# A fused attention and two-MLP kernel: the second MLP by seven block products in place of eight

## The chip, the cores and the metric

One NeuronCore of a Trainium2 chip runs the whole program. The metric is the device time of one execution in microseconds; the kernel before takes 1175.07 us (median of 3 runs, 1174.54 to 1177.42).

## What is computed

Four batches of eight heads of attention (576 positions, head size 64, scores masked to those within `tau` of the row's maximum), then two MLPs in float32 over 2304 tokens of width 512:

```python
x = attention(q, k, v, tau)                  # 2304 x 512
h = x @ w_in;  y = (h * sigmoid(h)) @ w_out  # 512 -> 2048 -> 512
out = ((y @ w_a) * (y @ w_b)) @ w_out2       # 512 -> 1536 -> 512
```

The MLP weights reach the kernel as 64-bit words (float64). They are turned on chip into a pair of float32r matrices, a high part and a low part, and each product is made of three matmuls: low weight by high activation, high by high, high weight by low activation.

## The kernel before

**Order of the work.** The body does not issue instructions directly. It records tasks in a planner (`Plan.add`) with an engine, a cost, a rank, what they wait for and which buffer ring they take, and `Plan.run` plays them through and so fixes the order in which each engine's instructions stand. On the chip every engine then takes its own list strictly in that order, and waits at an instruction until its inputs are there. Tasks of the second MLP's weights have the rank 1e6, so the plan puts them where an engine has nothing else.

**First MLP.** Tokens go in five blocks of 256 and two of 512 (`BLOCKS`), each in 16 steps of 128 hidden columns. `mlp1_up` does 12 matmuls into one PSUM bank (`hb` or `hc`), ACT takes tanh, DVE the gate `th` (L743), ACT the high part `gh`, DVE the low part `gl` (L749), and `mlp1_down` does 12 matmuls of the step before into the banks `yc` to `yf` or `sb`. At a block's end the result is halved, stored to DRAM as `yT_d` (L816) and read back by `load_y` of the second MLP. Blocks 0 to 3 run amid the attention; `closed` marks its end. Block 4 and the two big blocks come after it: the late part.

**Second MLP's weights.** `split_weight` makes one 128x512 piece at a time, 36 in all, from `closed` on: load, two ACT passes (low word L330, high part L354), DVE scale, sign and join (L337, L341, L346), an integer add of two words on POOL (L350) and the low part on POOL or DVE (L358). The pieces stay in SBUF, in the 32 tiles `w` that the first MLP's weights leave one by one, and in 4 more.

**Second MLP.** Tokens go in four blocks of 512 and one of 256. For each of 12 slices of 128 hidden columns `mlp2_up` does 24 matmuls of the block's width (L876, banks `ps_a` and `ps_b`); ACT copies a, DVE multiplies by b (L886), ACT and DVE split the product (L889, L892); `mlp2_down` does 3 matmuls of 512 columns for each 128 tokens (L920) into `op`. In all 1152 matmuls of 512 columns and 288 of 256 in the up part, 648 of 512 in the down part.

Of the kernel before, what the change touches and what calls it, by code (L numbers as in the profile page):

```python
# [21 lines left out]
P = 128  # L22
# [12 lines left out]
T2 = 512  # L35

# [178 lines left out]
def fused_kernel(ctx: ExitStack, tc: tile.TileContext, qk, qk2, v, tau, w_in, w_out, w_a, w_b, w_o2, out):  # L215
# [14 lines left out]
    yT_d = dram.tile([NC, P, NT], F32, name="yT_d")  # L230

# [3 lines left out]
    def pool(stack, name, bufs, side="left", **kw):  # L235
# [18 lines left out]
    xb_p = pool(p1, "xb", RINGS["xb"])  # L254
    g_p = pool(p1, "g", 2)
    yo_p = pool(p1, "yo", RINGS["yo"])
# [121 lines left out]

    def w1_chunk(i, rank):
        j, i = divmod(i, 8)  # L380
        engines = dict(scale_engine=SCALE_ON[i % len(SCALE_ON)], lo_engine=LO_ON[i % len(LO_ON)], most=PIECE)
        if i < 4:
            return split_weight(("in", i, j), w_in[i * P:(i + 1) * P, j * 512:(j + 1) * 512], rank, "w", **engines)
        f = 4 * j + i - 4
        return split_weight(("out", f), w_out[f * P:(f + 1) * P, :], rank, "w", **engines)
# [446 lines left out]
    y2, y2_ready, zs, z_ready, o_ps = {}, {}, {}, {}, {}  # L832

    def load_y(t0):
        tn = min(T2, NT - t0)
        need = [t for a, m, t in y_dma if a < t0 + tn and a + m > t0]
        ab = "ab"[t0 // T2 % 2]

        def split(c):
            s = {}  # L840

            def load():
                s["r"] = pools["ya"].tile([P, T2], F32, name="yr", bufs=RINGS["yr"])
                nc.sync.dma_start(out=s["r"][:, :tn], in_=yT_d[c, :, t0:t0 + tn])

            def hi():
                s["h"] = pools["y" + ab].tile([P, T2], F32R, name="yh" + ab)
                s["l"] = pools["y" + ab].tile([P, T2], F32R, name="yl" + ab)
                y2[t0, c] = (s["h"], s["l"])
                nc.scalar.copy(out=s["h"][:, :tn], in_=s["r"][:, :tn])  # L850

            def lo():
                nc.vector.tensor_sub(out=s["l"][:, :tn], in0=s["r"][:, :tn], in1=s["h"][:, :tn].bitcast(F32))

            ld = dma(-1, P * 4 * tn, load, after=[*need, closed], take=["yr"])
            h = pl.add("ACT", act_ns(tn), R_AUX, hi, [ld], ["y2" + ab], behind=[closed1] if ab == "b" else [])
            l = pl.add("DVE", dve_ns(tn), R_AUX, lo, [h])
            pl.free("yr", l)
            y2_ready[t0, c] = (h, l)

        for c in range(NC):
            split(c)

    def mlp2_up(n, t0, f):
        tn = min(T2, NT - t0)
        s = zs[t0, f] = {}

        def up(nm, c):
            def fn():
                if c == 0:  # L870
                    s[nm] = pools["ab", n % 2].tile([P, T2], F32, name=f"ps_{nm}")
                w = wt[nm, c, f // 4]
                o = (f % 4) * P
                yh, yl = y2[t0, c]
                for k, (a, yy) in enumerate(((1, yh), (0, yh), (0, yl))):
                    nc.tensor.matmul(s[nm][:, :tn], lhsT=w[:, a, o:o + P], rhs=yy[:, :tn],  # L876
                                     start=(c == 0 and k == 0), stop=(c == NC - 1 and k == 2))
            return fn
# [9 lines left out]
        def hi():  # L888
            nc.scalar.copy(out=s["zh"][:, :tn], in_=s["z"][:, :tn])  # L889
# [166 lines left out]
```

## Time and profile before

| what | value |
|---|---|
| median of 3 runs | 1175.07 us |
| span of the profiled execution | 1173.2 us |
| PE busy | 1142.9 us, 97% |
| DVE busy | 621.7 us, 53% |
| ACT busy | 531.1 us, 45% |
| POOL busy | 271.4 us, 23% |
| DMA traffic | 90.05 MB, mean 77 GB/s |

The profiled execution is given by its span, from its first to its last instruction; the run times are taken by another clock around the whole execution and lie 1.9 us above it at the median. A busy share is an average over stages: attention until about 497 us, the late part of the first MLP until about 725 us, the second MLP to the end. A matmul's record runs on after the next has started, so the pace of matmuls is read from their starts, not from their durations.

### The profile page before, as it was taken

To read this page: it belongs to the slowest core of one execution; us is meant where nothing else is said; L and a number is where in the kernel's file an instruction comes from. 1 tells how busy PE (TensorE), PEld (TensorE's weight loads), DVE (VectorE), ACT (ScalarE), POOL (GpSimd) and SP (SyncE) were. 2 spreads that over 40 slices of the span, in tenths; PEclk is the share of its full clock that TensorE was granted. 3 is DMA by queue.
4 is the path that set the end of the run, shared out by engine and by line. 5 is a ranking of instruction groups with operands and counts; after the bars stand their busy time and mean duration, and the time that the engine had idled before them with its cause. 6 is when DMAs were issued, how large, how long until landed. Compare 5 with 4: busy or idle time off the path is not lost.

```text
span 1173.2 us, 18253 instructions
## 1 busy us (share of the span) xinstructions
PE 1142.9 (97%) x6917; PEld 957.8 (82%) x6917; DVE 621.7 (53%) x1416; ACT 531.1 (45%) x999; POOL 271.4 (23%) x440
## 2 busy tenths in 40 slices
PE   8789989999999999999999999999999999999998
PEld 6456757988999989899888888888888888888897
DVE  8988887877777777463223678673211311211121
ACT  7877786666766766442223445442211211211121
POOL 2444444333322422140001344451000000000000
PEclk9999999999999999999999999999999999999999
DMA  6654543322322221150001235440100200000000
GB/s 199 199 163 138 163 155 109 113 88 79 107 73 84 82 95 35 36 190 18 1 1 45 88 111 167 140 138 13 63 1 1 68 0 1 23 28 1 1 36 18
DMA packets 41095, 90.05 MB, mean 77 GB/s; under 512 B 4256, under 2 KB 18224, under 8 KB 41008
## 3 DMA queue, kind: packets, MB, share of 16 engines
q1 hardware_dynamic: 40864, 88.89, 23.7%
q8 instruction: 54, 0.88, 0.3%
q14 instruction: 33, 0.27, 0.1%
q10 hardware_dynamic: 144, 0.00, 0.0%
HBM read 74.65 MB, written 14.23 MB: 76 GB/s over the span
## 4 chain that ended last, share of the span: by engine, by line
PE 60%; DMA 2%; DVE 1%; ACT 1%; issue 0%; POOL 0%; SPq 0%; ACTq 0%; POOLq 0%
PE ps_a L876 13%; PE op L920 13%; PE ps_b L876 13%; PE hb L730 5%; PE hc L730 4%; PE sb L790 3%; PE yc L790 2%; PE yd L790 1%; PE ye L790 1%; PE yf L790 1%; DMA wraw<-w_a 1%; PE av L605 1%; PE tp L560 1%; PE sa L495 1%; DMA wraw<-w_b 1%
## 5 line engine op out<-in xcount | busy, mean ns | idle before, releaser
L886 DVE TENSOR_TENSOR z<-ps_b,z 128x512 f32<-128x512 f32 (+1 forms) x60 | 38.2, 637 | 227.9 <-PE ps_b L876 227.8
L730 PE MATMUL hb<-xh,w 128*128 128x256 f32 (+1 forms) x704 | 155.2, 310 | 1.5 <-DVE th L743 1.0
L350 POOL TENSOR_TENSOR wt<-wc,wt 128x128 uint32<-128x128 uint32 (+1 forms) x164 | 111.2, 702 | 140.2 <-DVE wc L346 98.7
L920 PE MATMUL op<-w,zh 128*128 128x512 f32 x432 | 133.9, 391 | 0.0
L511 DVE TENSOR_SCALAR_CACHE_REDUCE t<-sa,nscale 128x576 f32<-128x576 f32 x128 | 103.7, 810 | 50.6 <-PE sa L495 45.6
L528 DVE SCALAR_TENSOR_TENSOR e<-t,thr,e 128x576 f32<-128x576 f32 x128 | 111.5, 871 | 26.4 <-ACT e L525 24.8
L730 PEld LDWEIGHTS hb<-xh,w 128*128 128x128 f32 x704 | 113.0, 190 | 10.9 <-issue 2.3
L560 PE MATMUL tp<-ident,e 128*128 128x128 f32 x706 | 106.2, 278 | 12.9 <-DVE e L528 8.3
L560 PEld LDWEIGHTS tp<-ident,e 128*128 128x128 f32 x706 | 78.7, 140 | 37.2 <-issue 14.7
L525 ACT ACTIVATE e<-t,min 128x576 f32<-128x576 f32 x128 | 99.9, 781 | 19.2 <-DVE t L511 18.5
L883 ACT COPY z<-ps_a 128x512 f32<-128x512 f32 (+1 forms) x60 | 32.6, 543 | 165.0 <-PE ps_a L876 165.0
L730 PE MATMUL hb<-xl,w 128*128 128x256 f32 (+1 forms) x352 | 106.5, 303 | 0.7 <-POOL xl L702 0.7
L790 PE MATMUL sb<-gh,w 128*128 128x256 f32 (+1 forms) x576 | 97.6, 300 | 0.0
L920 PEld LDWEIGHTS op<-w,zh 128*128 128x128 f32 x432 | 80.3, 188 | 16.4
L889 ACT CAST zh<-z 128x512 fp32r<-128x512 f32 (+1 forms) x60 | 34.7, 578 | 127.5 <-DVE z L886 127.5
L790 PEld LDWEIGHTS sb<-gh,w 128*128 128x128 f32 x576 | 80.0, 190 | 5.9 <-issue 3.3
L920 PE MATMUL op<-w,zl 128*128 128x512 f32 x216 | 84.6, 392 | 0.0
L749 DVE TENSOR_TENSOR gl<-th,gh 128x256 fp32r<-128x256 f32 (+1 forms) x112 | 63.9, 571 | 28.3 <-ACT gh L746 28.1
L876 PE MATMUL ps_a<-yha,w 128*128 128x512 f32 (+1 forms) x288 | 77.4, 355 | 0.0
L876 PE MATMUL ps_b<-yha,w 128*128 128x512 f32 (+1 forms) x288 | 77.0, 354 | 0.0
L640 POOL TENSOR_TENSOR x<-x,xi 128x128 f32<-128x128 f32 (+2 forms) x80 | 40.9, 535 | 147.1 <-issue 49.9
L702 POOL TENSOR_TENSOR xl<-xr,xh 128x128 fp32r<-128x128 f32 x72 | 37.0, 542 | 161.0 <-ACT xh L699 156.4
(123 smaller groups left out, 2342.8 us busy)
## 6 DMA issues: line engine op xcount, KB each, us to landing
qk<-qk SPq DMA_DIRECT2D x20, 576.0 KB
wraw<-w_in SPq DMA_DIRECT2D x16, 512.0 KB
wraw<-w_out SPq DMA_DIRECT2D x16, 512.0 KB
v<-v SPq DMA_DIRECT2D x20, 320.0 KB
wraw<-w_a SPq DMA_DIRECT2D x12, 512.0 KB
wraw<-w_b SPq DMA_DIRECT2D x12, 512.0 KB
wraw<-w_o SPq DMA_DIRECT2D x12, 512.0 KB
out<-ob SPq DMA_DIRECT2D x18, 256.0 KB
```

Of the source, the lines that this page charges most:

```text
L350: nc.gpsimd.tensor_tensor(out=s["t"][:, o], in0=s["c"][:, o].bitcast(U32), in1=s["t"][:, o], op=ALU.add)
L511: nc.vector.tensor_scalar(out=s["t"], in0=s["s"][:, :, :NH], scalar1=nscale, scalar2=None, op0=ALU.mult, op1=ALU.min, accum_out=s["min"])
L525: nc.scalar.activation(out=s["e"], in_=s["t"], func=AF.Exp, scale=-1.0, bias=s["min"])
L528: nc.vector.scalar_tensor_tensor(out=s["e"], in0=s["s"][:, :, :NH] if early else s["t"], scalar=s["thr"], in1=s["e"], op0=ALU.is_ge if ear ...
L560: nc.tensor.transpose(t["tp"][:, j * P:(j + 1) * P], e["e"][:, o:o + P], ident)
L640: nc.gpsimd.tensor_tensor(out=s["x"][:, o], in0=s["x"][:, o], in1=s["i"][:, o], op=ALU.mult)
L730: nc.tensor.matmul(s["h"], lhsT=w[:, a, o:o + P], rhs=xx, start=(c == 0 and k == 0), stop=(c == NC - 1 and k == 2))
L749: nc.vector.tensor_sub(out=s["gl"], in0=s["t"], in1=s["gh"].bitcast(F32))
L790: nc.tensor.matmul(ys[j][e // per][:, e % per * tn:(e % per + 1) * tn], lhsT=w[:, a, e * P:(e + 1) * P], rhs=gs[j, f][g], start=(f == 0 an ...
L876: nc.tensor.matmul(s[nm][:, :tn], lhsT=w[:, a, o:o + P], rhs=yy[:, :tn], start=(c == 0 and k == 0), stop=(c == NC - 1 and k == 2))
L886: nc.vector.tensor_mul(out=s["z"][:, :tn], in0=s["b"][:, :tn], in1=s["z"][:, :tn])
L920: nc.tensor.matmul(o_ps[t0, i], lhsT=s[z][:, i * P:(i + 1) * P], rhs=wt["o2", f][:, a, :], start=(f == 0 and k == 0), stop=(f == NF2 - 1 a ...
```

## The change

The second MLP is done with Strassen's scheme in Winograd's form. Both matrices of each product are cut in 2 x 2 blocks; seven products of block sums replace eight of blocks. A unit is 768 tokens, and its two halves are the even and the odd tokens, 384 each (`TN`).

- **Weights.** In place of 36 pieces there are 36 units of four blocks (`split_unit`): 24 for `w_a` and `w_b`, 12 for `w_out2`. ACT does three passes (L870, L873, L898), DVE everything else: sign, join, the integer add (`total`), three small sums (`combine`, `both`), and the low part of seven blocks (`lo`, 896 columns). POOL does none of it. The seven blocks, high and low, are stored to DRAM (`wab_d`, `wo_d`) by one DMA of 917,504 bytes that is cut in pieces of 512 bytes; the load is two DMAs in pieces of 1 KB. Units go through buffers `u` (two deep) and, in the big blocks, also `v`.
- **Stream.** For every product (up) or third of a product (down) 512 KB of weights, 4 KB a partition, are read back from DRAM into one of 12 tiles `ws`: 63 loads per unit of tokens, 189 in all.
- **Products.** `products` runs them in the order 1, 6, 5, 7, 2, 4, 3 over three pairs of PSUM banks and keeps partial sums in the banks. After 1 ACT copies a pair out; after 6, 7, 5, 4 and 3 DVE adds (`u2`, `v`, `c22`, `c21`, `c12`, 768 columns each). Product 7 waits for `u2`, 4 for `v`, 3 for `c22`. Each up product is 12 matmuls of 384 columns, each down product three times 12.
- **Token sums.** `load_y` reads 768 tokens at once and DVE makes four block sums; the seven operands are split by ACT and DVE (`halves`). In the down part each third of a product needs one such split, through rings `zh` and `zl` of two tiles.
- **Start.** `closed1`, which opens the second MLP's tiles, stands behind all 36 stores.
- **Output.** `out` is written transposed, and the host puts it in order.

```diff
+UNIT = 768
+TN = UNIT // 2
+NG = NF2 // 2
+ORDER = (1, 6, 5, 7, 2, 4, 3)
+CHAIN = {1: 0, 2: 0, 6: 1, 7: 1, 4: 1, 5: 2, 3: 2}
+PART = {1: 0, 4: 1, 2: 2, 5: 3, 6: 4, 7: 5, 3: 6}
+N_YW, N_SW, N_TW = 14, 12, 6
+SPARE = range(6, 30)
+LO2_ON = ("DVE",)
+TOTAL_ON = ("DVE",)
...
+    wab_d = dram.tile([NG, 7, P, 2, 4, P], F32, name="wab_d")
+    wo_d = dram.tile([7, NG // 2, P, 2, 2, 2, P], F32, name="wo_d")
...
+    def split_unit(key, src, dst, rank, lane, behind, lo_engine, total_engine):
...
+        def low():
+            s["a"] = new("s", [P, 8, P], F32)
+            nc.scalar.activation(out=s["a"][:, 4:].bitcast(U32), in_=s["raw"][:, :, :, 0], func=AF.Copy, scale=2.0**-29)
+
+        def scale():
+            nc.scalar.activation(out=s["a"][:, :4], in_=s["raw"][:, :, :, 1].bitcast(F32), func=AF.Copy, scale=2.0**-112)
+
+        def sign():
+            nc.vector.tensor_scalar(out=s["raw"][:, :, :, 1], in0=s["raw"][:, :, :, 1], scalar1=0x80000000, scalar2=None,
+                                    op0=ALU.bitwise_and)
+
+        def join():
+            c = s["a"][:, :4].bitcast(U32)
+            nc.vector.scalar_tensor_tensor(out=c, in0=c, scalar=3, in1=s["raw"][:, :, :, 1],
+                                           op0=ALU.logical_shift_left, op1=ALU.bitwise_or)
+
+        def total(o):
+            a = s["a"].rearrange("p a n -> p (a n)").bitcast(U32)
+            eng = nc.gpsimd if total_engine == "Pool" else nc.vector
+            eng.tensor_tensor(out=a[:, o], in0=a[:, o], in1=a[:, 512 + o.start:512 + o.stop], op=ALU.add)
+
+        def combine(o, x, y, op):
+            return lambda: nc.vector.tensor_tensor(out=s["a"][:, o], in0=s["a"][:, x], in1=s["a"][:, y], op=op)
+
+        def both():
+            a = s["a"]
+            nc.vector.tensor_tensor(out=a[:, 4:6], in0=a[:, 0:7:6], in1=a[:, 2:3].broadcast_to((P, 2, P)), op=ALU.add)
+
+        def hi():
+            s["w"] = new("w", [P, 2, 7, P], F32R)
+            nc.scalar.copy(out=s["w"][:, 0], in_=s["a"][:, 1:])
+
+        def lo():
+            eng = nc.gpsimd if lo_engine == "Pool" else nc.vector
+            eng.tensor_tensor(out=s["w"][:, 1], in0=s["a"][:, 1:], in1=s["w"][:, 0].bitcast(F32), op=ALU.subtract)
+
+        def store():
+            nc.sync.dma_start(out=dst.rearrange("i p l n -> p l i n"), in_=s["w"].bitcast(F32))
...
+        a = dma(rank, P * 4096, load, n=2, take=[lane + "r"], behind=behind)
+        l = pl.add("ACT", ac(512), rank, low, [a], take=[lane + "s"])
+        c = pl.add("ACT", ac(512), rank, scale, [a], behind=[l])
+        h = pl.add("DVE", 600, rank, sign, [a, c], port=True)
+        j = pl.add("DVE", dv(512), rank, join, [h, c], port=True)
+        pl.free(lane + "r", j, l)
+        if total_engine == "Pool":
+            t = on_pool(512, rank, total, [j, l], PIECE)[-1]
+        else:
+            t = pl.add("DVE", dv(512), rank, lambda: total(slice(0, 512)), [j, l], port=True)
+        t = pl.add("DVE", dv(P), rank, combine(6, 0, 1, ALU.subtract), [t], port=True)
+        t = pl.add("DVE", dv(2 * P), rank, both, [t], port=True)
+        t = pl.add("DVE", dv(P), rank, combine(7, 3, 5, ALU.subtract), [t], port=True)
+        i = pl.add("ACT", ac(7 * P), rank, hi, [t], [lane + "w"])
+        o = pl.add(lo_engine, pool_ns(7 * P) if lo_engine == "Pool" else dv(7 * P), rank, lo, [i], port=True)
+        pl.free(lane + "s", o)
+        st = dma(rank, P * 7168, store, after=[o], slack=SLACK)
+        pl.free(lane + "w", st)
+        stored[key] = st
+        return st
...
+            lane, behind = ("v", [closed_x]) if n % 3 == 2 and n in SPARE else ("u", [closed])
...
+    def stream(src, after):
+        s = {}
+
+        def load():
+            s["w"] = pools["ws"].tile([P, 2, 512], F32R, name="w")
+            nc.sync.dma_start(out=s["w"].bitcast(F32), in_=src)
+
+        s["ready"] = dma(1e4 + pe_at[0], P * 4096, load, after=after, take=["ws"])
+        return s
...
+    def products(s, do, after):
+
+        p, cost = {}, 12 * pe_ns(TN)
+        p1, u2, v, c22, c21, c12 = chain(s)
+        add = lambda fn, deps, take=(): pl.add("DVE", dv(UNIT), -3, fn, deps, take)
+        wait = {}
+        for i in ORDER:
+            take, behind, alloc = [], [], None
+            if i in (1, 6, 5):
+                alloc, behind = take_pair(s, CHAIN[i])
+                take = ["pr"]
+            for k, (fn, deps, done) in enumerate(do(i)):
+                def run(fn=fn, alloc=alloc if k == 0 else None):
+                    if alloc:
+                        alloc()
+                    fn()
+                p[i] = pe_task(cost, run, [*deps, *wait.get(i, ())], take if k == 0 else [], behind if k == 0 else [])
+                done(p[i])
+            if i == 1:
+                wait_p1 = pl.add("ACT", ac(UNIT), -3, p1, [p[1]], ["tm"], behind=[closed1])
+                wait[2] = [wait_p1]
+            elif i == 6:
+                s["u2"] = add(u2, [p[6], wait_p1], ["tm"])
+                wait[7] = [s["u2"]]
+            elif i == 7:
+                s["v"] = add(v, [p[7]], ["tm"])
+                s["c22"] = add(c22, [s["v"], p[5]])
+                wait[4], wait[3] = [s["v"]], [s["c22"]]
+            elif i == 2:
+                after(p[2])
+            elif i == 4:
+                s["c21"] = add(c21, [p[4], s["v"]])
+            elif i == 3:
+                s["c12"] = add(c12, [p[3]])
+        return p
...
+    def mlp2_up(u, g, y):
...
+                bank = s["b", CHAIN[i]]
+                for m in range(2):
+                    for k in range(2):
+                        for q, (a, x) in enumerate(((1, "h"), (0, "h"), (0, "l"))):
+                            nc.tensor.matmul(bank[:, m, :TN], lhsT=w["w"][:, a, (2 * m + k) * P:(2 * m + k + 1) * P],
+                                             rhs=y[i][x][:, k, :TN], start=(i in (1, 6, 5) and k == 0 and q == 0),
+                                             stop=(k == 1 and q == 2), skip_group_check=True)
+            yield fn, [w["ready"], *y[i]["ready"]], lambda p: pl.free("ws", p)
...
+    def mlp2_down(u):
...
+                z = halves(lambda k=k, sl=sl: zs[u, sl, k][:, :, :TN], TN,
+                           lambda: pools["zc"].tile([P, 2, TN], F32R, name="zh", bufs=RINGS["zh"]), "zh",
+                           lambda: pools["zc"].tile([P, 2, TN], F32R, name="zl", bufs=RINGS["zl"]), "zl",
+                           [zs[u, sl, "ready"][i]], 1e4 + pe_at[0] + sl)
...
+    closed_x = pl.add("none", 1, 0, close_small, behind=[small_done, closed])
...
+    closed_y = pl.add("none", 1, 0, close_spare, behind=prepare_weights())
+    closed1 = pl.add("none", 1, 0, close_mlp1,
+                     behind=[up_last[0], down_last[0], closed_x, closed_b, *stored.values(), *(t for *_, t in y_dma)])
+    for u in range(NT // UNIT):
+        y = load_y(u, pe_at[0])
+        for g in range(NG):
+            p = mlp2_up(u, g, y)
+        for i in ORDER:
+            pl.free("wy", p[i])
+            pl.free("wy", p[i])
+        mlp2_down(u)
```

How the engines' lists move, at three places. DVE, a step and a half of the first MLP's last block, in the kernel before (`th` is the gate, `gl` the low part; `wraw`, `wc`, `w` are a weight piece):

```order
L743 SCALAR_TENSOR_TENSOR th_8765<-th_8765,hc 128x512
L341 TENSOR_SCALAR wraw<-wraw 128x512
L749 TENSOR_TENSOR gl_8767<-th_8765,gh_8766 128x512
L346 SCALAR_TENSOR_TENSOR wc<-wc,wraw 128x512
L337 TENSOR_SCALAR wc<-wraw 128x512
L341 TENSOR_SCALAR wraw<-wraw 128x512
L358 TENSOR_TENSOR w<-wt,w 128x512
L743 SCALAR_TENSOR_TENSOR th_8814<-th_8814,hb 128x512
```

DVE in the same block now, from one gate to the next (`us`, `ur`, `uw` are one unit's buffers; the integer add is the row `ISA`):

```order
L760 SCALAR_TENSOR_TENSOR th_8837<-th_8837,hb 128x512
L894 TENSOR_TENSOR us<-us 128x256
L881 SCALAR_TENSOR_TENSOR us<-us,ur 128x512
L766 TENSOR_TENSOR gl_8839<-th_8837,gh_8838 128x512
L890 TENSOR_TENSOR us<-us 128x128
L887 ISA us<-us 128x1024
L890 TENSOR_TENSOR us<-us 128x128
L902 TENSOR_TENSOR uw<-us,uw 128x896
L894 TENSOR_TENSOR us<-us 128x256
L760 SCALAR_TENSOR_TENSOR th_8890<-th_8890,hc 128x512
```

Between two gates stand seven instructions of weights where five stood. The first of them in DVE's list comes right behind block 3's last evacuation; the last comes just ahead of the last step's gate. In between stand 36 units of weights, 31 gates and low parts of 512 columns, 15 and 16 of 256, 3 evacuations, and 11 operations of 768 columns on the first unit of tokens. Ahead of that place the lists of all engines are the same as before.

PE in the second MLP, one group of 128 + 128 hidden columns (`pr` are pairs of banks):

```order
L1120 MATMUL pr_9566<-w 128x384 x12
L1120 MATMUL pr_9584<-w 128x384 x12
L1120 MATMUL pr_9605<-w 128x384 x12
L1120 MATMUL pr_9584<-w 128x384 x12
L1120 MATMUL pr_9566<-w 128x384 x12
L1120 MATMUL pr_9584<-w 128x384 x12
L1120 MATMUL pr_9605<-w 128x384 x12
L1120 MATMUL pr_9694<-w 128x384 x12
```

The seven products follow each other with nothing between, 1512 matmuls in all; the down part has 756. Before, an up step of 24 matmuls and a down step of 12 took turns.

DVE in the down part of the first unit of tokens (`zl` is the low part of a product's operand):

```order
L975 TENSOR_TENSOR zl<-z_9428,zh 128x768
L1056 TENSOR_TENSOR tm<-pr_10143,tm 128x768
L975 TENSOR_TENSOR zl<-z_9675,zh 128x768
L1059 TENSOR_TENSOR tm<-pr_10215,tm 128x768
L975 TENSOR_TENSOR zl<-z_9922,zh 128x768
L975 TENSOR_TENSOR zl<-w,zh 128x768 x3
```

A low part now stands ahead of every 12 matmuls, with at most one other operation between two of them.

## Rows read from the trace of the kernel before

**Rows 1.** The page: span, busy time by engine, granted TensorE clock in 40 slices.

```profile
span 1173.2 us, 18253 instructions
PE 1142.9 (97%) x6917; PEld 957.8 (82%) x6917; DVE 621.7 (53%) x1416; ACT 531.1 (45%) x999; POOL 271.4 (23%) x440
PEclk9999999999999999999999999999999999999999
```

**Rows 2.** The chain that ended last, share of the span by engine.

```profile
PE 60%; DMA 2%; DVE 1%; ACT 1%; issue 0%; POOL 0%; SPq 0%; ACTq 0%; POOLq 0%
```

**Rows 3.** Busy time by stretch: PE, PEld, DVE, ACT, POOL, clock, DMA share, GB/s.

```profile
540.00:726.00 186.00, 185.95 (x859) 155.30 (x858) 88.94 (x133) 67.25 (x114) 38.72 (x38) 1.00 0.18 56
726.00:1169.00 443.00, 443.00 (x2081) 370.26 (x2079) 129.57 (x206) 100.60 (x179) 36.47 (x27) 1.00 0.12 39
```

**Rows 4.** Timeline of PE: the second MLP's first, a late first-MLP, the last matmul.

```profile
723.17 0.63 PE L876 MATMUL ps_a<-yha,w 128*128 128x512 f32 x2
...
723.87 0.40 PE L790 MATMUL yc<-gl,w 128*128 128x512 f32 x1
...
1168.97 0.39 PE L920 MATMUL op<-w,zl 128*128 128x512 f32 x1
```

**Rows 5.** Timeline of PE, block 4: two rows that lie 24 matmuls apart.

```profile
520.80 0.64 PE L790 MATMUL yc<-gh,w 128*128 128x256 f32 x4
...
523.68 0.64 PE L790 MATMUL yc<-gh,w 128*128 128x256 f32 x4
```

**Rows 6.** Groups by line and shape, DVE and ACT, 820 to 1160 us.

```profile
L892 DVE TENSOR_TENSOR zl<-z,zh 128x512 fp32r<-128x512 f32 x37 | 25.6, 693 | 23.4 <-ACT zh L889 23.3
L892 DVE TENSOR_TENSOR zl<-z,zh 128x256 fp32r<-128x256 f32 x10 | 4.2, 424 | 4.2 <-ACT zh L889 4.2
L889 ACT CAST zh<-z 128x512 fp32r<-128x512 f32 x36 | 22.4, 621 | 99.4 <-DVE z L886 99.4
L889 ACT CAST zh<-z 128x256 fp32r<-128x256 f32 x10 | 4.1, 406 | 14.7 <-DVE z L886 14.7
```

**Rows 7.** Timeline of DVE and POOL, 721 to 726 us.

```profile
721.20 1.83 DVE L749 TENSOR_TENSOR gl<-th,gh 128x512 fp32r<-128x512 f32 x1
721.19 1.29 POOL L350 TENSOR_TENSOR wt<-wc,wt 128x512 uint32<-128x512 uint32 x1 [1.56 <-DVE wc L346]
723.89 0.41 DVE L341 TENSOR_SCALAR wraw<-wraw 128x512 uint32<-128x512 uint32 x1
724.34 0.69 DVE L346 SCALAR_TENSOR_TENSOR wc<-wc,wraw 128x512 uint32<-128x512 uint32 x1
724.95 0.68 DVE L812 TENSOR_SCALAR yo<-yd 128x512 f32<-128x512 f32 x1
```

**Rows 8.** Timelines of SP, DVE and PE: the ends of the late part's stretches.

```profile
497.90 0.43 SPq L326 DMA_DIRECT2D wraw<-w_a  x1
505.95 0.69 DVE L812 TENSOR_SCALAR yo<-sb 128x512 f32<-128x512 f32 x1 [0.18 <-ACT yo L810]
718.06 0.39 PE L730 MATMUL hc<-xl,w 128*128 128x512 f32 x1
```

**Rows 9.** DMA, 545 to 560 us: two stores in 1 KB pieces (packets, MB, share).

```profile
q1 hardware_dynamic: 544, 0.52, 10.3%
```

**Rows 10.** DMA, 638 to 646 us: four stores in 2 KB pieces.

```profile
q1 hardware_dynamic: 576, 1.05, 35.1%
```

**Rows 11.** DMA, 488.2 to 489.2 us: one store of five 512-byte pieces.

```profile
q1 hardware_dynamic: 10, 0.00, 1.1%
```

**Rows 12.** DMA, 497.4 to 500 us: loads of 4 KB pieces, nearly alone.

```profile
q1 hardware_dynamic: 384, 0.70, 92.1%
```

**Rows 13.** DMA, 729 to 732 us: loads of 4 KB and 2 KB pieces, nearly alone.

```profile
q1 hardware_dynamic: 542, 1.16, 104.9%
```

**Rows 14.** Timelines of ACT and SP: the last evacuation and the last stores' issue.

```profile
1169.40 0.58 ACT L927 COPY ob<-op 128x512 f32<-128x512 f32 x1 [1.83 <-PE op L920]
1169.43 0.91 SPq L931 DMA_DIRECT2D out<-ob  x2
```

More of the change, by code (lines that the diff above doesn't have):

```diff
@@ L377, in split_weight, with w_pool @@
         return [a, l, c, h, j, *ts, i, *os]
+    def w_pool(k):
+        return "wy" if k < N_YW else "ws" if k < N_YW + N_SW else "wz"
     def w1_chunk(i, rank):
+        dst = w_pool(i)
         j, i = divmod(i, 8)
@@ L829, in mlp1_down @@
                 b_done.extend(evs[2:])
[L832 to L862, printed above, removed]
@@ new lines, in prepare_weights @@
+    def prepare_weights():
+        units = []
+        for g in range(NG):
+            for m, w in enumerate((w_a, w_b)):
+                for k in range(2):
+                    r = w.rearrange("(h k p) (e f) two -> h k p e f two", h=2, k=2, e=2)
+                    units.append(((m, k, g), [r[h, k, :, :, g * P:(g + 1) * P] for h in range(2)], wab_d[g, :, :, :, 2 * m + k]))
+        for g in range(NG):
+            for c in range(2):
+                r = w_o2.rearrange("(h g p) (e f) two -> h g p e f two", h=2, g=NG, e=2)
+                units.append((("o", g, c), [r[h, g, :, :, c * P:(c + 1) * P] for h in range(2)], wo_d[:, g // 2, :, :, g % 2, c]))
+        done = []
+        for n, unit in enumerate(units):
+            lane, behind = ("v", [closed_x]) if n % 3 == 2 and n in SPARE else ("u", [closed])
+            st = split_unit(*unit, 1e6 + n, lane, behind, LO2_ON[n % len(LO2_ON)], TOTAL_ON[n % len(TOTAL_ON)])
+            if lane == "v":
+                done.append(st)
+        return done
@@ new lines, in fused_kernel, with pe_task, load @@
+    pe_at = [0]
+    pe_last = [None]
+    def pe_task(cost, fn, after, take=(), behind=()):
+        pe_at[0] += 1
+        pe_last[0] = pl.add("PE", cost, 1e5 + pe_at[0], fn, after, take, behind=[pe_last[0], *behind])
+        return pe_last[0]
+    def stream(src, after):
+        s = {}
+        def load():
+            s["w"] = pools["ws"].tile([P, 2, 512], F32R, name="w")
+            nc.sync.dma_start(out=s["w"].bitcast(F32), in_=src)
+        s["ready"] = dma(1e4 + pe_at[0], P * 4096, load, after=after, take=["ws"])
+        return s
@@ new lines, in halves, with hi, lo @@
+    def halves(v, n, hi_pool, hi_take, lo_pool, lo_take, after, rank, behind=()):
+        s = {}
+        def hi():
+            s["h"] = hi_pool()
+            nc.scalar.copy(out=s["h"][:, :, :n], in_=v())
+        def lo():
+            s["l"] = lo_pool()
+            nc.vector.tensor_sub(out=s["l"][:, :, :n], in0=v(), in1=s["h"][:, :, :n].bitcast(F32))
+        h = pl.add("ACT", ac(2 * n), rank, hi, after, [hi_take], behind=behind)
+        l = pl.add("DVE", dv(2 * n), rank, lo, [h], [lo_take])
+        s["ready"] = [h, l]
+        return s
@@ L979, in fused_kernel, with close_small @@
             mlp1_down(n - 1, *units[n - 1])
+        if n and units[n - 1] == (4, NF - 1):
+            small_done = down_last[0]
     mlp1_down(n, *units[n])
-    for j in range(4):
-        for c in range(NC):
-            pl.free("w", w_last["in", c, j])
-        for f in range(4 * j, 4 * j + 4):
-            pl.free("w", w_last["out", f])
+    for k in range(32):
+        j, i = divmod(k, 8)
+        pl.free(w_pool(k), w_last[("in", i, j) if i < 4 else ("out", 4 * j + i - 4)])
+    def close_small():
+        p1x.close()
+        pools["v"] = pool(px, "v", 1)
```

295 lines of the change are left out of this document (190 added, 105 removed).

## The prediction

> **What bounds the kernel now.** I read the page first: PE is busy for 97% of the span, no other engine for more than 53%, and the granted clock stays at its upper level of 2.4 GHz in every slice [rows 1]. The chain of waits says the same: PE holds 60% of the span, nothing else over 2% [rows 2]. Shares of a whole program hide its stages, so I then took busy time by stretch. From 540 to 726 us PE is busy for 185.95 of 186 us, from 726 to 1169 us for all of it, while DVE is busy for 48% of the late part of the first MLP and 29% of the second [rows 3]. So fewer matmul columns in the second MLP come off the time one for one, as long as the work that the change puts on DVE and the DMA engines stays under PE's own time.
>
> **The matmuls.** From the first start to the last slot's end the second MLP takes 1169.20 - 723.17 = 446.0 us; four matmuls of the first MLP lie in it, 0.9 us [rows 4], so its own are 445.1. Matmuls of 256 columns follow each other every (523.68 - 520.80) / 24 = 0.120 us [rows 5]. The 288 of these cost 34.6, which leaves 410.5 / 1800 = 0.228 us for each of 512. A straight line through both gives 0.174 us at 384 columns; a width between two measured ones is a safe reading. There are 1512 + 756 = 2268 of them: 394.8 us. **Term: -50.3 us.** The list of PE has nothing between the products, so all of it is on the path.
>
> **Weights in the late part, on DVE.** A unit's seven instructions: sign 0.41, join 0.69 [rows 7]; three sums and the low part by the line through 0.424 (256 columns) and 0.693 (512) [rows 6], that is 0.289 twice, 0.424, and 1.10 for 896 columns; and the integer add. That add stands nowhere in the trace on DVE. From below it is another two-stream operation on 512 words, 0.69. From above it goes by the 1024 columns that the list gives it, 1.23 by the same line. I take 0.69, since join has the same words and streams. A unit is 3.89 us, 36 are 140.0. With 62 gates and low parts of 512 columns (42.8), 31 of 256 (13.1), 3 evacuations (2.1) and 11 operations of 768 columns on tokens (10.6) DVE has **208.6 us** to do between block 3's evacuation and the last step's gate. In the kernel before that stretch goes from 506.6 to about 719.2 us (0.25 us for the matmul to drain and 0.6 for tanh behind the last up matmul at 718.06) [rows 8], 212.6 us. That is 98%, and every microsecond over it delays a gate, the last down step and all that follows. For it: POOL falls silent, and the long DVE records of today, 1.83 us for a low part, lie beside POOL's [rows 7]. Against: DVE takes its list in order and must also wait for loads and ACT. A step leaves about 3 us between the low part and the matmul that needs it, which hides single delays. **Term: +6 us**, from 0 up to 26 (below).
>
> Here a rule speaks otherwise than my sum. My line has a fixed part of 0.155 us an instruction; but three rows in turn start at 724.34 and 724.95, 0.61 us apart where the first lasts 0.69 [rows 7], so neighbours that don't need each other overlap by 0.08. Over 359 instructions this is up to 29 us, and the need is 180 us. The Trainium skill (Vector Engine (DVE) Microarchitecture Reference, section 5.2) states 1.0417 ns a column plus about 75 ns per instruction after queue overlap, which gives the same 180 us. I stay between, because within a unit each operation needs the one before: from sign's end to join's start the rows show a gap of 0.04.
>
> **Weights in the late part, on the DMA engines.** Time of 16 engines: 1 KB pieces cost 0.103 x 16 x 15 us / 512 = 48.3 ns [rows 9], 2 KB pieces 0.351 x 16 x 8 / 512 = 87.7 ns [rows 10], a line that gives 28.6 ns at 512 bytes. One store of five such pieces shows at most 35 ns [rows 11]; the upper bound is the price of 1 KB. The stores are 36 x 1792 = 64,512 pieces, 4032 for each engine: 115 us at 28.6 ns, 141 at 35, 195 at 48.3. Loads add 18,432 pieces of 1 KB, 55.6 us; other transfers some 34. Together 205, 231 or 284 us against 228 us from the first weight load at 497.90 [rows 8] to the second MLP. I take 28.6 ns, the line's value, 90%: hidden, but close.
>
> **The stream in the second MLP.** Twelve matmuls last 2.09 us and need 512 KB. Loads of 4 KB pieces took 38.3 us of engine time for 0.70 MB [rows 12], 1.79 us for 512 KB; beside those of 2 KB pieces 50.4 us for 1.16 MB [rows 13], 1.42 us. With token loads and stores this is 70 to 92%; twelve tiles, 25 us of work, cover swings. Nothing.
>
> **DVE and ACT in the second MLP.** A group of 14.6 us holds five adds of 0.96, four products of 0.56 and, every second time, four sums of 0.96: 9 us. An add that product 7 or 4 waits for has one product of 2.09 us to cover 0.25 + 0.96. In the down part the split has two buffers: it starts when the product before last is done, and needs 0.25 + 0.84 (ACT, line through 0.406 and 0.621 [rows 6]) + 0.96 + some 0.14 of hand-overs = 2.19 us; it has 2.09 plus two matmuls of 0.174, since the low part comes third. Slack 0.24, so a second DVE operation in a gap can cost a little. **Term: +2 us**, from 0 to 23 (24 other operations of 0.96).
>
> **The end.** Today 4.0 us pass from the last matmul's slot to the end, with an evacuation of 0.58 and two stores of 256 KB [rows 14]; then an add of 0.96 and one of 393 KB. **Term: +1 us**, from 0 to 2. All before 497 us stays: the lists are the same.
>
> **Sum.** -50.3 + 6 + 2 + 1 = -41.3: span 1173.2 - 41.3 = 1131.9. The median of the runs lies 1.9 above this execution's span, so **1134 us** for the runs.
>
> **Rivals.** All replace one term of the sum.
> - *DVE isn't full*: with the overlap of 0.08 the 6 us vanish, 1128. For it, the three rows above; against, chains within a unit.
> - *DVE decides the late part*: the integer add goes by half words (36 x 0.54 = 19.4) and the 252 weight instructions each wait 0.04 (10.1): 238.1 for 212.6, 25.5 us in place of 6, 1153. Against: no two-stream row on DVE costs more than its columns.
> - *The down part waits*: every other DVE operation pushes a low part by its length, 23 us in place of 2, 1155. Against: in the list at most one stands between two low parts, and a gap of 2.09 - 0.96 holds one.
> - *The matmul doesn't get shorter as it says*: weight loads are busy for 370.26 / 2079 = 0.178 us each [rows 3]; if that were a floor, 2268 x 0.178 = 403.7 and the time is 1143. Against: 256 columns run at 0.120.
> - *Slower, the 512-byte stores*: at 48.3 ns a piece the DMA engines need 284 us for 228, so stores hold the `u` buffers, ACT waits for them ahead of tanh, and PE waits for ACT: 56 us in place of 6, **1184**. It decides from 34.3 ns, where the sum is 228; the time of today comes back at 46. For it: nothing in the trace runs such pieces in bulk. Against: the line, and the 35 ns of the only five.
>
> **Chances.** Forecast 0.45, DVE not full 0.22, DVE full 0.13, down part waits 0.09, pace 0.03, DMA stores 0.08. The measurement tells 0.3% from no change. All cases but the last end faster, and a little of their far ends touches no change: faster 0.91, same 0.02, slower 0.07. The range goes from 1124, all terms but the first at nothing, to 1160, which takes in DVE and the down part at their bounds, and leaves out the DMA case.
>
> **What would show it.** Right: 1512 matmuls of the up part 0.174 us apart, the second MLP's first matmul at 724 to 732 us, some 395 us from there to the last, POOL idle after the attention, DVE over 90% busy in the late part. The integer add's mean, 0.7 or 1.2, and the pieces' price from 510 to 720 us tell the rivals apart; PE waiting for ACT or DVE there means the late part was too full, PE idle ahead of L1206 that the down part waits. I am wrong if the second MLP takes over 402 us, or starts after 745.

## The result, and the profile after

The changed kernel takes 1141.25 us (median of four runs, 1140.41 to 1144.45) against 1174.83 us for the kernel before, a ratio of 0.971 with a 95% interval of 0.9687 to 0.9732. The forecast was 1134 us with a range of 1124 to 1160. So the direction and the range held, and 7 of the 41 us that were forecast as gain did not come. The profiled execution is the longest of the four: 1144.45 us with a span of 1142.6. The ratios leave out one slow execution, of 2744.38 us, of the kernel with less work on DVE below.

The page of the changed kernel, beside [rows 1] and [rows 2]:

```profile
span 1142.6 us, 19524 instructions
PE 1105.2 (97%) x7097; PEld 985.2 (86%) x7097; DVE 822.8 (72%) x1702; ACT 574.1 (50%) x1012; POOL 201.9 (18%) x386
PEclk9989999999999999999999899999999999999999
```

PE is still the engine that bounds, and DVE has gone from 53% to 72%. Two slices of the clock are below the top: the third, where nothing is changed, and the 23rd, 628 to 657 us, which is new. Busy time by stretch shows what lies there (columns as in [rows 3]: PE, PEld, DVE, ACT, POOL, granted clock, DMA share, GB/s):

```profile
540.00:640.00 100.00, 100.00 (x476) 83.16 (x476) 84.16 (x165) 62.19 (x101) 3.70 (x8) 1.00 0.94 274
640.00:660.00 20.00, 15.70 (x58) 12.33 (x57) 14.80 (x30) 10.91 (x18) 2.03 (x4) 0.83 0.96 289
660.00:736.00 76.00, 76.00 (x334) 62.36 (x333) 63.23 (x109) 39.11 (x60) 0.00 (x0) 1.00 0.92 293
736.00:1138.00 402.00, 397.06 (x2269) 393.77 (x2267) 246.56 (x296) 91.87 (x120) 0.00 (x0) 1.00 0.79 249
```

Two places are not full. From 640 to 660 us PE loses 4.3 us and the clock falls to 0.83; in the second MLP PE loses 4.9 us. DVE is busy for 162.2 of the 196 us from 540 to 736, 83%; my sum had 98%, and had counted on over 90% as a sign of being right. The DMA engines are at 0.92 to 0.96. The list of waits of PE, from 498 us to the second MLP and from there to the end, names each loss (total us, times, longest):

```profile
PE yc L807 <- ACT gh L763: 4.9, 2, 4.3
PE pr L1206 <- DVE zl L975: 4.8, 7, 2.5
```

The timeline of PE gives the borders: the first product of block 5's down part into `ye`, the first of the second MLP, and the last matmul.

```profile
556.94 0.63 PE L807 MATMUL ye<-gh,w 128*128 128x512 f32 x2
...
735.87 2.42 PE L1120 MATMUL pr<-w 128*128 128x384 f32 x13
...
1137.88 0.34 PE L1206 MATMUL pr<-zl,w 128*128 128x384 f32 x1
```

The second MLP takes 1138.05 - 735.87 = 402.2 us, where 445.1 stood and 396.8 was forecast. It starts at 735.87 us, where 724 to 732 was the sign of being right, and 11.8 us later than in the kernel before (724.1 when the four late matmuls of [rows 4] are taken off), where 6 was forecast. Of these 11.8 us, 2.9 lie ahead of block 4 (its first down product starts at 508.41 us; before, at 505.47), where the change does nothing; in the changed kernel run again below it starts at 505.74, and over all the traces it lies between 503.5 and 510.2. Another -1.1 lies in block 4. From block 5's `ye` to the second MLP it is 178.9 us against 169.0: the change costs **9.9 us** there.

**The border of blocks 5 and 6.** The timelines of ACT, DVE and PE:

```profile
642.54 0.60 ACT L827 ACTIVATE yo<-ye 128x512 f32<-128x512 f32 x1 [0.93 <-PE ye L807]
646.30 0.60 ACT L827 ACTIVATE yo<-sb 128x512 f32<-128x512 f32 x1 [3.17 <-DMA yT_d<-yo]
646.80 0.93 ACT L898 CAST vw<-vs 128x896 fp32r<-128x896 f32 x1
647.63 0.60 ACT L757 ACTIVATE th<-hb 128x512 f32<-128x512 f32 x1
650.33 0.62 ACT L763 CAST gh<-th 128x512 fp32r<-128x512 f32 x1 [0.23 <-DVE th L760]
...
647.76 1.09 DVE L902 TENSOR_TENSOR vw<-vs,vw 128x896 fp32r<-128x896 f32 x1 [1.69 <-ACT vw L898]
649.01 0.69 DVE L829 TENSOR_SCALAR yo<-sb 128x512 f32<-128x512 f32 x1 [0.15 <-DMA yT_d<-yo]
649.62 0.68 DVE L760 SCALAR_TENSOR_TENSOR th<-th,hb 128x512 f32<-128x512 f32 x1
...
651.00 1.22 PE L807 MATMUL yc<-gh,w 128*128 128x512 f32 x2 [4.30 <-ACT gh L763]
652.02 1.05 PE L807 MATMUL yd<-gh,w 128*128 128x512 f32 x2
652.87 1.05 PE L807 MATMUL ye<-gh,w 128*128 128x512 f32 x2
```

Block 5 has four output tiles and two `yo` buffers. ACT's copy of `sb` is third, so it waits 3.17 us for the first tile's store to land. Behind it in ACT's list stand a cast of weights and then the first tanh of block 6; behind that DVE's gate, ACT's `gh`, and PE. DVE adds a part of its own: tanh ends at 648.23 us, but a low part of weights and the copy of `sb` stand ahead of the gate, which starts 1.4 us later. After the stop of 4.3 us the matmuls come every 0.43 us: the granted clock is at the lower level, 1.2 GHz, from 651 to 656 us, which costs 2.5 us more.

### The profile page after: what moved, and what is told of

Same layout as the page of the kernel before. It is cut to its first block, busy times and chain, and to the rows that moved or that the text cites. A ratio compares the mean times of both kernels' runs of the same rounds, so it can differ in the third digit from the quotient of the medians.

```text
span 1142.6 us, 19524 instructions
## 1 busy us (share of the span) xinstructions
PE 1105.2 (97%) x7097; PEld 985.2 (86%) x7097; DVE 822.8 (72%) x1702; ACT 574.1 (50%) x1012; POOL 201.9 (18%) x386
## 4 chain that ended last, share of the span: by engine, by line
PE 81%; DMA 7%; DVE 5%; ACT 4%; issue 2%; POOL 1%; SPq 0%; POOLq 0%; DVEq 0%; ACTq 0%
PE pr L1120 23%; PE hb L747 11%; PE pr L1206 9%; PE sb L807 8%; PE av L622 6%; PE tp L577 5%; PE hc L747 5%; PE sa L512 4%; PE yc L807 2%; PE yd L807 2%; PE ye L807 2%; PE yf L807 2%; DMA wraw<-w_out 1%; DMA xi<-r_d 1%; DMA wraw<-w_in 1%
## 5 line engine op out<-in xcount | busy, mean ns | idle before, releaser
L1120 PE MATMUL pr<-w 128*128 128x384 f32 x1512 | 262.6, 334 | 0.0
L1120 PEld LDWEIGHTS pr<-w 128*128 128x128 f32 x1512 | 262.2, 188 | 0.1
L1206 PE MATMUL pr<-zh,w 128*128 128x384 f32 x504 | 129.2, 338 | 0.0
L1206 PEld LDWEIGHTS pr<-zh,w 128*128 128x128 f32 x504 | 91.9, 190 | 0.0
L1206 PE MATMUL pr<-zl,w 128*128 128x384 f32 x252 | 86.4, 343 | 4.9 <-DVE zl L975 4.8
L971 ACT CAST zh<-z 128x768 fp32r<-128x768 f32 x45 | 37.5, 833 | 84.1 <-PE pr L1206 58.4
L363 POOL TENSOR_TENSOR wt<-wc,wt 128x128 uint32<-128x128 uint32 x128 | 62.3, 517 | 77.3 <-DVE wc L359 48.4
L747 PEld LDWEIGHTS hb<-xl,w 128*128 128x128 f32 x352 | 67.1, 191 | 3.7 <-POOL xl L719 0.9
L512 PE MATMUL sa<-sp 128*128 128x288 f32 (+1 forms) x400 | 69.9, 300 | 0.0
L584 ACT COPY pb<-tp 128x512 f32<-128x512 f32 (+2 forms) x128 | 60.3, 493 | 17.7 <-PE tp L577 17.5
```

What stands on the lines that cost most here:

```text
L363: nc.gpsimd.tensor_tensor(out=s["t"][:, o], in0=s["c"][:, o].bitcast(U32), in1=s["t"][:, o], op=ALU.add)
L512: nc.tensor.matmul(s["s"][:r + m, j, :NH], lhsT=hd["t"][:, 0, c - r:c + m], rhs=hd["t"][:, k, j * NH:(j + 1) * NH], start=(k == 1), stop=( ...
L584: nc.scalar.copy(out=dst(s["p"]), in_=t["tp"][:, :m * P] if m < 4 else t["tp"].rearrange("p (k q) -> p k q", k=4))
L747: nc.tensor.matmul(s["h"], lhsT=w[:, a, o:o + P], rhs=xx, start=(c == 0 and k == 0), stop=(c == NC - 1 and k == 2))
L1120: nc.tensor.matmul(bank[:, m, :TN], lhsT=w["w"][:, a, (2 * m + k) * P:(2 * m + k + 1) * P], rhs=y[i][x][:, k, :TN], start=(i in (1, 6, 5) ...
L1206: nc.tensor.matmul(bank[:, c, :TN], lhsT=w["w"][:, a, (2 * e + c) * P:(2 * e + c + 1) * P], rhs=z[x][:, e], start=(i in (1, 6, 5) and sl = ...
```

## The experiments

Theory A: the late part slips at this border because the weights' stores fill the DMA engines. Theory B: it slips because DVE's list is nearly full, as I had forecast. Theories C and D are about the second MLP's waits.

In the code cuts, `...` stands for lines left out.

**Leave out most of the stores.** Only 8 of the 36 units are stored.

```diff
+        if key[1 if key[0] == "o" else 2] > (1 if key[0] == "o" else 0):
+            pl.free(lane + "w", o)
+            return o
         st = dma(rank, P * 7168, store, after=[o], slack=SLACK)
...
```

> 28 of the 36 stores of combined weights are left out (the stream then reads the first chunk's weights every time), everything else of the preparation stays: loads, ACT and DVE work. Theory A (the late part slips because the stores fill the DMA engines, so that the store of the first MLP's output lands late, ACT's next copy of sb waits for its buffer, and tanh and TensorE wait behind that): the wait of 4.3 us at 646 us goes, the first product matmul starts at 725 to 728 us instead of 735.87, time 1130 to 1134 us. Theory B (the slip comes from DVE, whose list is nearly full): start stays at 733 to 737, time 1138 to 1142. If the slower pace of TensorE in block 5 (0.2333 us a matmul against 0.2267 before) comes from the stores too, it returns to 0.227; if from the loads or from DVE and ACT, it stays.

Measured: 1139.97 us, ratio 0.9698 (0.9682 to 0.9714), no gain that can be told, where theory A had 1130 to 1134. From `ye` to the second MLP it is 177.0 us (178.9 in the change). The DMA share from 560 to 640 us fell to 0.33 and the wait for the `yo` store to 0.66 us, but the planner had put the preparation of block 6's x elsewhere: ACT's last cast of x stood behind its first copy of the output, POOL's low parts followed, and PE stopped for them:

```profile
642.22 0.50 PE L747 MATMUL hb<-xl,w 128*128 128x512 f32 x1 [2.48 <-POOL xl L719]
```

What follows: with fewer transfers the wait for the store is shorter, 0.66 us for 3.17, yet PE stops at the same border for another thing that is late. B isn't tested by this run.

**Take work off DVE.**

```diff
-        h = pl.add("DVE", 600, rank, sign, [a, c], port=True)
...
-        t = pl.add("DVE", dv(P), rank, combine(7, 3, 5, ALU.subtract), [t], port=True)
...
+        pl.free(lane + "r", c, l)
...
```

> DVE makes only the low halves (1.10 us a unit, 36 units) and leaves out the sign, the join, the integer add and the three sums (2.8 us a unit); loads, ACT work and all stores stay, so the weights are not the right ones. Theory A (stores fill the DMA engines): start of the second MLP stays at 732 to 738 us, time 1138 to 1143. Theory B (DVE's list): start at 725 to 728, time 1130 to 1134. The pace of TensorE in block 5: back to 0.227 us a matmul if DVE's work slows it, 0.233 if the transfers do.

Measured: slower than the change, ratio 0.9768 (0.9745 to 0.9791); 183.5 us from `ye` to the second MLP. The stretches (columns as above):

```profile
560.00:640.00 80.00, 77.53 (x337) 62.73 (x336) 37.84 (x46) 55.17 (x87) 4.78 (x8) 1.00 1.05 312
640.00:660.00 20.00, 16.07 (x58) 12.21 (x57) 8.93 (x11) 12.11 (x20) 1.70 (x4) 0.83 1.06 319
```

DVE is at 47% and PE loses more time than in the change. Units now follow each other faster, and the DMA share goes to 1.05. In this run ACT waits 21.7 us in all for buffers of weights whose stores have not landed, where it waits for them at most 0.2 us in the change; its cast of a unit needs ACT's own two passes alone here, and so comes up sooner. At the border such a wait stands ahead of the copy and of the cast of x that PE needs:

```profile
644.03 0.94 ACT L898 CAST vw<-vs 128x896 fp32r<-128x896 f32 x1 [1.37 <-DMA wab_d<-vw]
644.88 0.59 ACT L827 ACTIVATE yo<-ye 128x512 f32<-128x512 f32 x1
645.37 0.61 ACT L716 CAST xh<-xr 128x512 fp32r<-128x512 f32 x1
...
646.02 1.22 PE L747 MATMUL hb<-xh,w 128*128 128x512 f32 x2 [3.38 <-ACT xh L716]
```

So less work on DVE doesn't help as long as the transfers and ACT's list hold PE. The run replaced one limit by another (that of my slow rival), so it can't say what DVE's list cost in the change. The kernel with the border late alone, below, can: there DVE does all its work, and PE stops for 1.3 us in place of 4.3.

**One more buffer at the border.**

```diff
...
-            outs = ("yo", "yo", "th5", "xr5") if last else ("yo",) * NC
+            outs = ("yo", "yo", "th5", "xr5") if last else ("yo", "yo", "yo5", "yo") if j == 5 else ("yo",) * NC
```

> Block 5's third output tile has a buffer of its own, so ACT's copy of sb waits for no store. Theory A: the waits of 3.2 us of ACT and 4.3 us of TensorE at 646 us, and the drop of the clock behind them, go: start of the second MLP 735.87 - 4.3 - 2.5 = 729, time about 1136 in the profiled run (1134 to 1138). Theory B, or if the slip is spread over the list: the time is made up by waits elsewhere, start 733 to 736, time 1139 to 1142.

Measured: ratio 0.9681 (0.9667 to 0.9696), and 175.2 us from `ye`, 3.7 less. ACT no longer waits, and the clock stays at 1.00, but DVE's copy, the fourth, waits for a store in front of the gate:

```profile
645.03 0.69 DVE L829 TENSOR_SCALAR yo<-sb 128x512 f32<-128x512 f32 x1 [1.48 <-DMA yT_d<-yo]
646.98 0.68 DVE L760 SCALAR_TENSOR_TENSOR th<-th,hb 128x512 f32<-128x512 f32 x1
```

and PE still stops for 2.9 us. Part of the wait moved to DVE, and behind it two weight instructions stand ahead of the gate (645.64 to 647 us). The second MLP starts at 730.89 us, between the two theories.

**Token sums later.** In the second MLP's first down part the timeline of DVE and PE in the change reads:

```profile
841.39 0.96 DVE L1007 TENSOR_TENSOR yt<-yr 128x768 f32<-128x768 f32 x1 [2.25 <-DMA yr<-yT_d]
842.38 0.96 DVE L1007 TENSOR_TENSOR yt<-yr,yt 128x768 f32<-128x768 f32 x1
843.26 0.95 DVE L975 TENSOR_TENSOR zl<-z,zh 128x768 fp32r<-128x768 f32 x1
...
844.27 0.69 PE L1206 MATMUL pr<-zl,w 128*128 128x384 f32 x1 [2.47 <-DVE zl L975]
```

DVE stands 2.25 us for the next unit's tokens, with a low part behind it that PE needs. The experiment tells the planner that this load lands 6 us later:

```diff
-            ld.append(dma(-1, P * 8 * UNIT, load(k), after=[*need, *ld], take=["yr"] if k == 0 else [], behind=[closed_y]))
+            ld.append(dma(-1, P * 8 * UNIT, load(k), after=[*need, *ld], take=["yr"] if k == 0 else [], behind=[closed_y], slack=6000 if u else 0))
```

> The planner takes the load of the next unit's tokens to land 6 us later, so that DVE's sums of these tokens (L1007) stand later in its list, behind low parts zl of the down part. Theory C (the sums wait for the load, and the low parts behind them make TensorE wait): the wait of 2.5 us at 844 us and the drop of the clock behind it go, the waits for zl fall from 4.8 us to 2 to 2.5, the second MLP from 402.2 to about 398.5, time 1137 to 1139. Theory D (two buffers of zh and zl make the waits, wherever the sums stand): the waits stay at 4 to 5 us, time 1140 to 1142.

Measured: ratio 0.9663 (0.9649 to 0.9678), clear of the change's interval. The waits for `zl` are 2.3 us, and the second MLP lasts from 730.82 to 1129.19, 398.4 us. Theory C is shown for the waits that went, with the buffers as they were; whether the two buffers make the 2.3 us that are left was not tested. The border was as bad as ever (4.6 us), so the two waits are apart.

**The change again, and stores in 1-KB pieces.**

> The changed kernel again, on the chip of the next three runs, to compare them with. Theory A says that the wait at the border of blocks 5 and 6 (4.3 us) and the pace of 0.2333 us a matmul in block 5 belong to the kernel and come again; the 2.9 us by which its block 4 began later than before's came in the first 84 us, where nothing is changed, and need not come again. Time 1140 to 1143 us.

Measured: 1139.89 us, just under the range, ratio 0.9716 (0.9689 to 0.9743); the border's stop is 4.4 us, `ye` to the second MLP 178.7, the second MLP 400.3.

```diff
-    wab_d = dram.tile([NG, 7, P, 2, 4, P], F32, name="wab_d")
+    wab_d = dram.tile([NG, 7, P, 4, 2, P], F32, name="wab_d")
...
-            nc.sync.dma_start(out=dst.rearrange("i p l n -> p l i n"), in_=s["w"].bitcast(F32))
+            nc.sync.dma_start(out=dst.rearrange("i p l n -> p i l n"), in_=s["w"].bitcast(F32))
...
```

> The combined weights lie in DRAM with low and high half next to each other, so that a store goes in 1024-byte pieces, not 512 (half as many, same bytes). By the measured 29.3 and 50.4 ns a piece the 36 stores take 101.6 us of the 16 engines in place of 118.1, 16.5 less. Theory A: the DMA share of 0.90 to 1.04 in block 5 falls by about 0.1, the wait at the border of blocks 5 and 6 shrinks to 1 to 3 us, the second MLP starts 2 to 5 us earlier than in the repeated changed kernel, time 1136 to 1139. Theory E (total DMA time does not decide, only the order of the lists at that border does): under 1 us of change, or a change with the sign of the reordering.

Measured: ratio 0.9718 (0.9688 to 0.9748), no change. The DMA answer for 560 to 640 us (packets, MB, share of 16 engines), first of the change, then of this kernel:

```profile
q1 hardware_dynamic: 35807, 22.25, 95.1%
```

```profile
q1 hardware_dynamic: 22719, 22.60, 86.1%
```

About the same bytes take 9 points less of the engines, and the border's stop is 4.3 us as before. Theory E holds against that part of A: a tenth of the load more or less decides nothing. That the order of the lists decides is shown by the border runs below.

**Almost no preparation.** Only 8 of 36 units are made.

```diff
         for n, unit in enumerate(units):
+            if n >= 4 and not 24 <= n < 28:
+                continue
...
```

> Only 8 of the 36 weight units are prepared at all; loads, ACT and DVE work and stores of the other 28 are left out (the stream reads the first chunk's weights). Floor of the late part: no wait at the border of blocks 5 and 6, second MLP starts at 720 to 726 us, time 1126 to 1133. If the pace of 0.2333 us in block 5 comes from the preparation's traffic on SBUF, it is 0.227 here; if it belongs to the kernel's instructions or their phase, it stays at 0.2333 or takes another of the three levels seen.

Measured: 1135.25 us, ratio 0.9665 (0.9643 to 0.9687), no stop at the border, and 173.6 us from `ye` to the second MLP, which starts at 729.41. So the floor that I had expected, a start at 720 to 726 and 1126 to 1133 us, was too low. The 173.6 are 4.6 us more than before the change, with 28 of the 36 units gone. It is the pace of the matmuls, to which I come below.

**Border and sums late, with and without 1-KB stores.** The border's edit is one word for the planner: it takes block 5's output stores to land 4 us later, so the copies of `sb`, which need their buffers, come to stand behind the first tanh of block 6.

```diff
-                st = dma(-1, P * 4 * T2, store(k), after=[ev])
+                st = dma(-1, P * 4 * T2, store(k), after=[ev], slack=4000 if j == 5 else 0)
```

> 1-KB stores, the token sums planned 6 us later, and the output stores of block 5 planned to land 4 us later, so that the copies of sb that need their buffers stand behind the tanh work in ACT's and DVE's lists. Theory A with C: no TensorE wait over 1 us at the border of blocks 5 and 6 and no drop of the clock there, waits for zl at 2 to 2.5 us; second MLP from 727 to 730, time 1130 to 1134. If only C holds: 1135 to 1137, as in the run with late sums alone.

> Only the output stores of block 5 are planned to land 4 us later (512-byte weight stores and the token sums as in the change), so the copies of sb stand behind the first tanh work of block 6 in ACT's and DVE's lists. Theory A: the wait of 4.3 to 4.4 us at the border goes down to 1 to 1.5 us and the clock does not fall there: start of the second MLP 4 to 6 us earlier against block 5's start than in the change, time 0.4% under it (ratio to before 0.966 to 0.969). Theory E (the 16 DMA engines' load itself costs it): the wait stays over 3 us, ratio 0.970 to 0.973.

> Border stores and token sums both planned late, weight stores still in 512-byte pieces. If the two waits are apart from each other, the gains add: ratio to before 0.962 to 0.966, and equal within 0.15% to the run with 1-KB stores beside it, since the transfers are hidden in either. If the size of the pieces decides, the kernel with 1-KB stores is faster by over 0.2%.

> 1-KB stores, sums and border stores late, again, beside the run without the 1-KB stores on one chip: ratio 0.962 to 0.966, 1130 to 1134 us.

Measured:

| kernel | ratio to before, interval | median us | stop at the border | `ye` to second MLP | second MLP |
|---|---|---|---|---|---|
| 1-KB stores, both late | 0.966 (0.9643 to 0.9676) | 1133.43 | 1.3 | 173.6 | 398.4 |
| border late alone | 0.9667 (0.9633 to 0.97) | 1135.64 | 1.3 | 173.6 | 399.5 |
| both late, 512-byte stores | 0.9648 (0.9622 to 0.9674) | 1133.51 | 1.3 | 173.6 | 398.4 |
| 1-KB stores, both late, again | 0.9645 (0.9619 to 0.9671) | 1132.9 | 1.3 | 173.6 | 398.4 |

With the border late alone, the timeline of ACT and of PE:

```profile
640.73 0.59 ACT L757 ACTIVATE th<-hb 128x512 f32<-128x512 f32 x1
642.58 0.62 ACT L763 CAST gh<-th 128x512 fp32r<-128x512 f32 x1
643.96 0.58 ACT L827 ACTIVATE yo<-sb 128x512 f32<-128x512 f32 x1
...
643.25 0.74 PE L807 MATMUL yc<-gh,w 128*128 128x512 f32 x2 [1.31 <-ACT gh L763]
```

and the stretches there, with the DMA share as high as ever:

```profile
560.00:640.00 80.00, 80.00 (x345) 64.79 (x344) 67.09 (x132) 47.84 (x76) 5.73 (x12) 1.00 0.95 276
640.00:660.00 20.00, 18.69 (x82) 15.01 (x81) 19.63 (x38) 12.96 (x20) 0.00 (x0) 1.00 1.00 298
```

The copy waits for nothing, the stop is 1.3 us, the clock stays up: 178.7 us of the change run again become 173.6, 5.1 of the 9.9, with all the weights' work and the DMA share at 0.95 to 1.00. What is left over the kernel before, 4.6 us, is the stop of 1.3 and some 3.3 of slower pace; DVE's list can cost no more than that stop there. Its times alone don't set it apart from the change (the intervals overlap); the trace does. With both edits the interval lies clear of the change's, and 1-KB pieces add nothing (0.9645 beside 0.9648 on one chip). This version, some 1133 us, is faster than both kernels.

**One stop on purpose.** The edit stands on the kernel with 1-KB stores and both late.

```diff
...
+        if u == (5, 3):
+            mlp1_down(n - 1, *units[n - 1])
+            mlp1_up(n, *u, late=[down_last[0]])
+            continue
```

> One time, at the fourth step of block 5, the down product is put ahead of the next up product, so that TensorE must wait once for the tanh chain (1 to 3 us). Theory F (the pace of 512-column matmuls holds one level until TensorE stops, and is found anew after a stop): 0.2333 us a matmul before the stop and 0.229 after it, to the end of block 5; the stop is paid back by some 1.4 us. Theory G (the pace belongs to block 5's instructions and tiles): 0.2333 on both sides of the stop.

Measured: ratio 0.9669 (0.9634 to 0.9704). The new order made PE wait nowhere in block 5, so neither theory was tested. PE stopped for 1.9 us at the border instead, and the pace went from 0.2333 to 0.229 there.

## Why the prediction was right or wrong

**Right: the term that carries it.** 402.2 us, less 4.8 of waits and 1.5 of lower clock behind the wait at 844 us, are 395.9 for 2268 matmuls, 0.1746 each, beside the 0.174 and 394.8 of the line. The rival with a floor of 0.178 falls.

**Right: the prices.** The integer add is one instruction of 0.68 us, the lower bound that I took:

```profile
643.71 0.68 DVE L887 CUSTOM_DVE_ANT_0 us<-us 128x1024 uint16<-128x1024 uint16 x1
```

A 512-byte piece costs, in a stretch of the change (677 to 679 us) with nothing else in it, 1.017 x 16 x 2 us / 1134 = 28.7 ns, where the line gave 28.6:

```profile
q1 hardware_dynamic: 1134, 0.58, 101.7%
```

"Hidden, but close" held for the sum of the transfers: the DMA engines were at 0.92 to 0.96. The slow rival, stores that take 56 us more, falls; but its chain, an ACT that waits for a store ahead of tanh, is what happened, in small and by another buffer. The rival in which DVE decides falls with the price of the add.

**Wrong: the 6 us of the late part.** The step that failed is "98%, and every microsecond over it delays a gate". The same 359 operations last 210.0 us in the changed kernel's trace when their durations are added up, for the 208.6 of my sum; but neighbours overlap, by 0.06 us on average, and together they cover 187.5 us of the 222.5 from the first of them to the last gate, 84%. So the prices were right and adding them up was wrong. An estimate from the figures of the Trainium skill (Vector Engine (DVE) Microarchitecture Reference, section 5.2) is 189 us when every operation goes column for column, and the 180 that I gave for it when the sign has half its columns, as its 0.41 us suggest; the trace lies between the two. I had seen the overlap and kept half of my own figure. The rival "DVE isn't full" was right about DVE, and wrong in that the 6 us would vanish. In place of DVE's sum stand three things that no term had: the stop at the border 4.3, the clock after it 2.5, and a slower first MLP, 384 x (0.2333 - 0.2267) = 2.5 us in block 5 and 360 x (0.229 - 0.2267) = 0.8 in block 6. They add up to 10.1 us; the 9.9 are less, as the kernel before lost 0.3 us of its own in that stretch. That a term of 6 stood in the sum for the 9.9 measured is luck, since its reason was another. I had costed the transfers as a total and never asked which waiting instruction would stand ahead of tanh when a store comes late.

**Wrong: the waits of the second MLP.** "+2" were 6.3 us in the profiled execution and 4.2 in the run again. The step that failed is "a second DVE operation in a gap can cost a little": the operation didn't only take its 0.96 us, it stood 2.25 us for its load, with the low part behind it. With the sums planned later the waits are 2.3 us, near the forecast's size, though no run shows that they come as I had it. I had set myself 402 us as the bound of being wrong: the profiled execution is just over it at 402.2, the one in the run again under it at 400.3.

**The end**: from the last slot at 1138.05 us to 1142.6 it is 4.6 us, 0.6 more than before for the 1 forecast.

**The sum**: in the change run again the span is 1137.8, 5.9 over the forecast: -0.8 ahead of block 5, 3.7 in the late part (9.7 for 6), 3.5 in the second MLP (400.3 for 396.8), -0.4 at the end, all rounded. The total came near because the large term was right; the two that missed erred the same way.

## What to carry to other kernels

When work is hidden beside the bounding engine, a sum of busy times that fits is not enough: go through the in-order lists at the stage borders, find each instruction that waits for a DMA, and see what the bounding engine needs from behind it. Moving such an instruction behind the urgent one gave 5.1 us here, with no byte and no operation less, while halving the number of DMA pieces gave nothing and taking 2.8 us a unit off DVE made it slower. An instruction that waits for a load costs its followers the wait on top of its own length.

## What the runs showed that I had not expected

**Matmuls of one shape have several paces.** Three timelines of PE, where rows of two or three matmuls tell the distance. Before the change, block 5, 0.68 us for three, 0.2267 each:

```profile
602.01 0.62 PE L730 MATMUL hb<-xh,w 128*128 128x512 f32 x2
...
602.69 0.62 PE L730 MATMUL hb<-xh,w 128*128 128x512 f32 x2
```

In the change, block 5 has 0.70 us for three, 0.2333; block 6, after the stop, 2.75 us for twelve, 0.229:

```profile
600.34 0.63 PE L747 MATMUL hc<-xh,w 128*128 128x512 f32 x2
...
601.04 0.63 PE L747 MATMUL hc<-xh,w 128*128 128x512 f32 x2
...
700.16 0.62 PE L747 MATMUL hb<-xh,w 128*128 128x512 f32 x2
...
702.91 0.62 PE L807 MATMUL yc<-gh,w 128*128 128x512 f32 x2
```

With almost no preparation, and no stop at the border, block 6 keeps 0.2333:

```profile
700.01 0.63 PE L747 MATMUL hc<-xh,w 128*128 128x512 f32 x2
...
700.71 0.63 PE L747 MATMUL hc<-xh,w 128*128 128x512 f32 x2
```

So neither the bulk of the transfers nor that of DVE's work is needed for the slower pace. In the run with little DVE work the pace changed in the middle of block 5, at a stop of 1.1 us at 561 us, from 0.2333 to 0.229. In all thirteen traces of the changed kernel and its versions block 5 begins with 0.2333, and the pace changes only where PE had stopped. That a stop causes it is not shown, since no stop was placed at will; why 0.2267 held before the change is open. At 0.2267 the best version would gain an estimated 3.3 us more, the 2.5 and 0.8 above.

**The clock.** It fell to its lower level after stops of 4.3 us (the border) and 2.47 us (844 us in the change), and after the 2.48 and 2.36 us of the run with few stores and the 3.38 and 2.28 us of the one with little DVE work; it did not after 2.91 us (at the border, with the third buffer), after 3.1 us (a wait for `zl` in the run with 1-KB stores alone), after 2.25 us (with almost no preparation), nor after 1.9 or 1.3 us. The length of the stop alone doesn't decide.
